# Linear attention and two squared-ReLU layers on one core: waits for finished weights, a sum of copies on DVE, operands moved by 16 bytes

## The chip, the cores and the metric

One core of a Trainium2 chip runs the kernel. The metric is the time of one execution on the device in microseconds: 1520.22 us is the median of three runs of the kernel before (1519.58 to 1520.62).

## The reference

Attention with a softmax over the head dimension of q and over the sequence of k, then two feed-forward layers. Inputs are float32: q, k, v of 8 x 8 x 576 x 64, and for each layer w_in of 512 x 2048 and w_out of 2048 x 512.

```python
q_s = softmax(q, axis=-1)
k_s = softmax(k, axis=2)
kv = np.einsum('bhsd,bhse->bhde', k_s, v)
x = np.einsum('bhsd,bhde->bhse', q_s, kv)
x = x.transpose(0, 2, 1, 3).reshape(4608, 512)
h = np.maximum(x @ w_in, 0.0)
x = h * h @ w_out
r = np.maximum(x @ w_in2, 0.0)
return r * r @ w_out2
```

## The kernel before, in words

**Tiling.** The 4608 tokens are 9 blocks of 512 (`NB`). The four matrix products are four stages one after the other: stage 0 takes attention and the first w_in, block by block; stage 1 the first w_out; stage 2 the second w_in; stage 3 the second w_out. Hidden activations go to DRAM and come back as tiles G. Each fp32 operand is split into a rounded high part and the rest, and each product is three matmuls: low by high, high by low, high by high (`passes`, L437 to L442; every such matmul has line L441).

**Seven products.** In stage 0 from the seventh block on (`FIRST = 6`), and in stages 1 to 3, the blocks of a product are combined by sums into seven products instead of eight (`LEFT`, `RIGHT`, `ORDER`). One operand tile then holds 2 x 7 pieces of 256 columns: seven high, seven low. `first_mm` (L450) makes the products of stages 0 and 2, whose outputs the trace calls n and m: a unit is seven products of 12 matmuls, and product 2 comes first and is the only one that reads piece 0 of the moving operand (`RIGHT[2] = 0`). There are four units in a block. `second_mm` (L498) makes those of stages 1 and 3 (both are y): 42 matmuls for each of eight parts a of each block. In stage 1 the weights W are stationary and G moves; in stage 3 G is stationary and W moves.

**Addresses.** Tiles whose name begins with G, x or v have 48 spare words, and `comb_hi` (L108) starts the pieces at a word offset in them: `PLAIN` 8 as a rule, `EARLY` 4 for `G0_0_0` and for the first x block, `LATE` 40 for all tiles G of stage 3 and 44 for its first two. A word is 4 bytes. The tile v is the moving operand of the seventh to ninth blocks in stage 0.

**After the products.** `first` (L986) joins the seven: ACT copies products 2 and 5 out of PSUM (`copy`, L468), POOL adds the two copies (`both`, L471), DVE subtracts the sum from product 1 (`rest`, L474), and the rest follows by `plain`, `summed`, `relu` and `square`. `second` (L1039) uses `both` and `rest` as well.

**Who decides the order.** All steps are made as operations with an engine, a cost and a due time; `schedule` (L594) simulates them, each engine taking the ready operation with the earliest due time whose tiles are free, and the resulting order is the program: every engine works through its own instructions in that order, and SP issues nearly all DMAs from one queue. A random search of 400 rounds moves due times of the first part only (up to a chunk of the third block). An `after` of the planner binds the chip only where the data do: a DMA that the planner puts behind another transfer for reasons of traffic alone waits for nothing on the chip.

**Weights.** For 13 parts the finished operand (1792 KB) is written to DRAM early (`keep`) and read back by `get_operand` (L183) from POOL's queue. `behind` (L794) names, for four of these reads, a load of activations that the planner puts ahead: `(2, 2)` and `(2, 3)` behind the last G of stage 1, `(3, 5)` and `(3, 7)` behind the fifth and the seventh G of stage 3. `load_g` (L494) reads G, `load_y` (L535) reads the output of stage 1 as xq, `load_raw` (L129) reads unconverted weights, and `between` (L1113) makes the x of stage 2, on POOL from the third block on.

Of the kernel before, what the change touches and what calls it, by code (L numbers as in the profile page):

```python
# [9 lines left out]
F32 = mybir.dt.float32  # L10
# [11 lines left out]
P = 128  # L22
# [26 lines left out]
def linear_attention_two_relu2_ffn(ctx: ExitStack, tc: tile.TileContext, q0, k0, eye, qh, kh, vh, wio, out):  # L49
# [27 lines left out]
    def f32(ap):  # L77
        return ap.bitcast(F32)
# [11 lines left out]
        return pool.tile([P, 2, HB], F32, name=name, tag=f"t{place.slot}")  # L90


    hls, cfs = {}, {}


    def comb_add(key, q, x, eng, new):
# [11 lines left out]
    def comb_hi(key, q, x, tag):  # L108
        if key not in hls:
            if key[0] in "Gxv":  # L110
                t = pool.tile([P, 14 * HB + SHIFT], F32R, name=key, tag=tag)
                o = LATE + 4 * (key in ("G1_0_0", "G1_0_1")) if key[:2] == "G1" else EARLY if key == "G0_0_0" or key[:2] == "x0" else PLAIN
                hls[key] = t[:, o:o + 14 * HB].rearrange("p (a b n) -> p a b n", a=2, b=7)
            else:
                hls[key] = pool.tile([P, 2, 7, HB], F32R, name=key, tag=tag)
        r, src = (slice(0, 2), q[:, 0:4:3]) if x == 0 else (slice(2, 7), cfs[key])
        nc.scalar.activation(out=hls[key][:, 0, r], in_=src, func=AF.Copy)  # L117

    def comb_lo(key, q, x):
        r, src = (slice(0, 2), q[:, 0:4:3]) if x == 0 else (slice(2, 7), cfs.pop(key))  # L120
        hl = hls[key]
        nc.vector.tensor_tensor(out=hl[:, 1, r], in0=src, in1=f32(hl[:, 0, r]), op=ALU.subtract)  # L122

# [53 lines left out]

    def put_operand(f, a):  # L180
        nc.sync.dma_start(out=ready_w[f, a], in_=f32(hls.pop(f"S{f}_{a}")))

    def get_operand(f, a, tag):  # L183
        hls[f"W{f}_{a}"] = pool.tile([P, 2, 7, HB], F32R, name=f"W{f}_{a}", tag=tag)
# [265 lines left out]
    def first_mm(l, j, u, i, place):  # L450

        k, o = (l, j, u), BANK[i]
        if i == o:
            m[k, o] = bank(place, f"{'nm'[l]}{i}_{j}_{u}")
        for s in range(2):
            w = hls[f"W{2 * l}_{2 * u + s}"]
            terms = []
            for kk in range(2):
                x, c = hls[f"{'vx'[l]}{j}_{kk}"], slice(kk * P, (kk + 1) * P)
                terms.append((w[:, 0, LEFT[i], c], w[:, 1, LEFT[i], c], x[:, 0, RIGHT[i]], x[:, 1, RIGHT[i]]))  # L460
            passes(m[k, o][:, s], terms, start=i == o and s == 0)

    def temp(k, i):
# [3 lines left out]
    def copy(k, i):  # L467
        nc.scalar.activation(out=temp(k, f"s{i}"), in_=m[k, i], func=AF.Copy)  # L468

    def both(k):  # L470
        nc.gpsimd.tensor_tensor(out=t[k, "s5"], in0=t[k, "s5"], in1=t[k, "s2"], op=ALU.add)  # L471

    def rest(k):
        nc.vector.tensor_tensor(out=t[k, "s5"], in0=m[k, 1], in1=t[k, "s5"], op=ALU.subtract)  # L474
# [71 lines left out]
    class Op:  # L546
        def __init__(self, eng, cost, due, fn, after, uses, lands, lag, port):
            self.eng, self.cost, self.due, self.fn, self.lands = eng, cost, due, fn, lands
            self.after = [a for a in after if a is not None]
            self.uses, self.lag, self.port = uses, lag, port  # L550
            self.start, self.group = None, group[0]
            self.next = []

    class Place:
# [33 lines left out]
    OVERLAP = {"DVE": 80, "ACT": 95, "POOL": 40}  # L588
    LAG, SLACK, HEAD, REST, COLD, SLOTS = 90, 1500, 110_000, 1600, 1400, {"t": TS, "ps": 8}

    def dma(due, fn, kb, after=(), uses=(), n=1):
        return op("SP", (570 if after else 390) * n, due, fn, after, uses, lands=kb)

    def schedule(moved, until=None):  # L594
        for o in ops:
# [17 lines left out]
        for x, o in enumerate(ops):  # L613
            o.rank = (o.due + moved.get(o.group, 0.0) + moved.get(x, 0.0), x)
            if not o.wait and (until is None or o.due < until.due + 60_000):
                push(0.0, "ready", o)
        done = []
        while events:
            now = events[0][0]
# [2 lines left out]
            while events and events[0][0] <= now:  # L622
                _, _, kind, what = heapq.heappop(events)
                if kind == "ready":
                    heapq.heappush(ready[what.eng], (what.rank, what))
                elif kind == "idle":
                    idle[what] = True
                else:
                    for x in what.uses:
                        x.users -= 1  # L630
                        if not x.users:
                            free[x.tag].append(x.slot)
                    for y in what.next:
                        y.wait -= 1

                        over = what.eng != y.eng or now < HEAD and any(b.eng != y.eng for b in y.after)
                        y.ready = max(y.ready, now + (LAG + y.lag if over else 0))
                        if not y.wait:
                            push(y.ready, "ready", y)
            for e, q in ready.items():  # L640
                held = []
                while idle[e] and q:
# [109 lines left out]
    def converted(f, a, h, due, raw, wf):  # L752

        (rp, rnew), (wp, wnew) = raw, wf
        l = dma(due - 8000, lambda: load_raw(f, a, h, rnew), 512, [], [rp])
        late = 2500 if f else 0
        c = op("ACT", act(512) + 40, due - 3000, lambda: low_word(f, a, h), [l], [rp], lag=late)
        g = op("DVE", 430, due - 2900, lambda: high_word(f, a, h), [l], [rp], lag=late, port=True)
        x = op("ACT", act(512) + 40, due - 1900, lambda: scaled(f, a, h, wnew), [g], [rp, wp])
        return op("DVE", 690, due - 700, lambda: join(f, a, h), [c, x], [rp, wp], port=True)  # L760
# [30 lines left out]
    def slot_of(a):  # L791
        return f"w{(a + 5) % 8}"

    g_loads, behind = {}, {(2, 2): (0, NB - 1, 7), (2, 3): (0, NB - 1, 7), (3, 5): (1, 0, 4), (3, 7): (1, 0, 6)}  # L794

    def weights(f, a, due):

        if (f, a) in KEPT:
            place = Place(slot_of(a))
            l = op("POOL", 1400, due - 9000, lambda: get_operand(f, a, slot_of(a)), [*kept[f, a], g_loads.get(behind.get((f, a))), begun.get((f, a))], [place], lands=1792, port=False)  # L800
            combined[f"W{f}_{a}"] = [l], place
            return
        beside = Place(slot_of(a + 1)) if f == 0 and a not in (2, 7) else None
# [182 lines left out]
    def first(l, j, u):  # L986
# [28 lines left out]
        c2 = copy_of(2, d + g)  # L1015
        mm(5, d + g, [M[2]])
        c5 = copy_of(5, d + 2 * g)
        s = op("POOL", gps(512), d + 3 * g, lambda: both(k), [c2, c5], [tt["s5"], tt["s2"]])
        mm(1, d + 4 * g, [M[5], *chain[-1:]])
        if (l, j, u) == (1, 0, 1):  # L1020
            begun[2, 7] = M[1]
# [65 lines left out]
    def hidden(l, j, a):  # L1087
# [13 lines left out]
        if n < 5 or n >= end - 6:  # L1101
            cf = cf_place(("cf", "att2")[n % 2])
        elif n % 3 == 2:
            cf = Place("cfx", parent=spare[l])
            cf = cf, lambda: spare[l].area(2048, 5 * HB).rearrange("p (a n) -> p a n", n=HB)
        else:
            cf = cf_place(("cf", "att2")[n % 3])
        y = g_loads[l, j, a] = dma(d - (30000 if n < 5 else 20000), lambda: load_g(l, j, a, new), 512, stored[l, j, a], [place])
        if l == 0:
            y = op("ACT", act(1024), d - 10000, lambda: g_square(j, a), [y], [place])  # L1110
# [2 lines left out]
    def between(j, kk):  # L1113
        d = when(2, j)
        tag = (("qx", "qa") if j == 0 else ("qc", "qd"))[kk]
        place = Place(tag)
        ld = dma(d - 20000, lambda: load_y(j, kk, tag), 512, [y_stored[(0, j), q] for q in range(4)], [place])
        combine(f"x{j}_{kk}", f"hl{(2 * j + kk + 3) % 4}", d - 10000 + 5000 * kk, ("DVE" if j < 2 else "POOL",) * 3, lambda: xq[j, kk], place, [ld], *cf_place("att1" if j == 0 else ("cf", "att2")[kk]))

    for j in range(NB):  # L1120
# [103 lines left out]
```

## Time and profile before

| what | value |
|---|---|
| median of three runs | 1520.22 us (1519.58 to 1520.62) |
| the profiled execution's own time | 1531.24 us |
| its span | 1529.4 us |
| PE busy | 1503.5 us (98%) |
| DVE, ACT, POOL busy | 1192.1, 966.5, 253.1 us |
| mean granted TensorE clock | 0.999 |

The span runs from the first to the last instruction; the execution's own time is 1.84 us longer. The profiled execution is 11.0 us longer than the median of the runs. Engine times overlap: the sum over engines says nothing, and an engine that is not on the path may wait at no cost. A row of the timeline gives start, duration, engine, line, operation, tiles, count, and in brackets the idle time ahead of it with what ended it.

### The profile page before, as it was taken

The page shows a single profiled execution, that of the slowest core. Times are in us where ns is not written, and L with a number is a line of the kernel's source. Part 1 is how long each engine was busy: PE and PEld are TensorE (multiplying, and loading weights), DVE is VectorE, ACT ScalarE, POOL GpSimd, SP SyncE. Part 2 cuts the span into 40 slices and gives each one's busy share as a digit, 9 for nine tenths or more (in the row PEclk, how much of TensorE's full clock was granted, in tenths as well). Part 3 has the DMA queues.
Part 4 walks back from the last instruction along what each step waited for, and adds up shares of the span by engine and source line. Part 5 has one row for each costly group of instructions (what it writes and reads, how often), then busy time and mean ns, then how long its engine had stood idle before and what let it go on. Part 6 is the DMA issues. An engine that isn't in the chain of part 4 may idle for free.

```text
span 1529.4 us, 30550 instructions
## 1 busy us (share of the span) xinstructions
PE 1503.5 (98%) x12036; PEld 1428.4 (93%) x12036; DVE 1192.1 (78%) x1819; ACT 966.5 (63%) x1617; POOL 253.1 (17%) x193
## 2 busy tenths in 40 slices
PE   7999999999999999999999999999999999999998
PEld 5788888889899999999998999999999999999998
DVE  7998777797977999999987544444455998898885
ACT  8987666686866666666555777777776434334332
POOL 1000000001110111111112433333211111111110
PEclk9999999999999999999999999999999999999999
DMA  9888999985669544444357767767659444433441
GB/s 371 291 294 314 345 322 323 346 277 195 194 208 327 175 140 139 138 139 139 123 203 287 242 216 229 244 205 236 222 171 359 160 134 130 136 129 130 137 128 46
DMA packets 154143, 326.63 MB, mean 214 GB/s; under 512 B 13072, under 2 KB 84880, under 8 KB 151184
## 3 DMA queue, kind: packets, MB, share of 16 engines
q1 hardware_dynamic: 152128, 300.83, 58.8%
q0 software_dynamic: 1872, 23.86, 4.2%
q8 instruction: 94, 1.54, 0.4%
q14 instruction: 49, 0.40, 0.1%
HBM read 189.63 MB, written 135.00 MB: 212 GB/s over the span
## 4 chain that ended last, share of the span: by engine, by line
PE 86%; issue 5%; DVE 3%; DMA 3%; ACT 3%; POOL 0%; SPq 0%; DVEq 0%; ACTq 0%; POOLq 0%
PE y L441 41%; PE m L441 21%; PE h L441 15%; PE n L441 6%; PE xps L398 1%; DMA xq<-y 1%; PE kvps L327 1%; DMA g<-t 1%; POOL ts L471 0%; ACT wf L159 0%; ACT w L150 0%; DMA w<-wio 0%; DMA w<-k 0%; DVE wf L164 0%; ACT w L215 0%
## 5 line engine op out<-in xcount | busy, mean ns | idle before, releaser
L441 PE MATMUL y<-W,G 128*128 128x256 f32 x3024 | 355.8, 281 | 1.2 <-DVE ts L474 1.2
L441 PEld LDWEIGHTS y<-W,G 128*128 128x128 f32 x3024 | 355.3, 189 | 1.4 <-DVE ts L474 1.4
L441 PE MATMUL m<-x,W 128*128 128x256 f32 x3024 | 345.8, 277 | 1.5 <-ACT ts L468 1.5
L441 PEld LDWEIGHTS m<-x,W 128*128 128x128 f32 x3024 | 345.1, 188 | 1.9 <-ACT ts L468 1.9
L441 PE MATMUL y<-G,W 128*128 128x256 f32 x3024 | 344.2, 276 | 2.2 <-DVE G L122 2.2
L441 PEld LDWEIGHTS y<-G,W 128*128 128x128 f32 x3024 | 343.4, 188 | 2.6 <-DVE G L122 2.6
L441 PE MATMUL h<-hl,w 128*128 128x512 f32 x1080 | 259.8, 396 | 3.4 <-DVE w L84 3.4
L441 PEld LDWEIGHTS h<-hl,w 128*128 128x128 f32 x1080 | 200.4, 188 | 49.6 <-DVE w L84 5.7
L471 POOL TENSOR_TENSOR ts<-ts,ts 128x512 f32<-128x512 f32 x65 | 100.6, 1548 | 782.5 <-DVE t L510 450.0
L117 ACT ACTIVATE G<-hl 128x1280 fp32r<-128x1280 f32 (+1 forms) x95 | 86.1, 925 | 120.9 <-PE y L441 61.6
L480 DVE TENSOR_TENSOR t<-m,ts 128x512 f32<-128x512 f32 x72 | 48.9, 688 | 116.2 <-PE m L441 89.4
L441 PE MATMUL n<-v,W 128*128 128x256 f32 x1008 | 124.5, 285 | 3.0 <-ACT t L477 3.0
L441 PEld LDWEIGHTS n<-v,W 128*128 128x128 f32 x1008 | 121.1, 191 | 5.9 <-ACT t L477 4.2
L122 DVE TENSOR_TENSOR G<-hl,G 128x512 fp32r<-128x512 f32 (+1 forms) x95 | 109.9, 1160 | 20.3 <-ACT G L117 19.1
L483 ACT ACTIVATE t<-t 128x512 f32<-128x512 f32 x96 | 59.6, 627 | 59.3 <-DVE t L480 58.1
L486 ACT ACTIVATE t<-t 128x512 f32<-128x512 f32 x144 | 88.8, 627 | 1.9
L122 DVE TENSOR_TENSOR G<-cf,G 128x1280 fp32r<-128x1280 f32 x51 | 79.7, 1563 | 7.7 <-ACT G L117 7.0
L122 DVE TENSOR_TENSOR G<-att,G 128x1280 fp32r<-128x1280 f32 x49 | 76.7, 1565 | 8.8 <-ACT G L117 8.3
L312 POOL PARTITION_ALL_REDUCE m<-m x28 | 26.2, 935 | 305.3 <-DVE m L308 156.9
L428 ACT ACTIVATE r<-h 128x512 f32<-128x512 f32 x96 | 56.7, 592 | 21.7 <-PE h L441 16.3
L117 ACT ACTIVATE G<-cf 128x1280 fp32r<-128x1280 f32 x51 | 64.4, 1263 | 7.7 <-DVE cf L106 7.7
L513 POOL TENSOR_TENSOR t<-t,t 128x512 f32<-128x512 f32 x34 | 62.1, 1849 | 42.1 <-DVE t L480 42.1
(195 smaller groups left out, 1880.6 us busy)
## 6 DMA issues: line engine op xcount, KB each, us to landing
g<-t SPq DMA_DIRECT2D x192, 256.0 KB, 4.0
hl<-g SPq DMA_DIRECT2D x51, 512.0 KB, 3.7
raw<-wio SPq DMA_DIRECT2D x48, 512.0 KB, 5.1
g<-r SPq DMA_DIRECT2D x96, 256.0 KB, 5.2
W<-o POOLq DMA_DIRECT2D x13, 1792.0 KB, 9.7
y<-t SPq DMA_DIRECT2D x72, 256.0 KB, 2.4
w<-wf SPq DMA_DIRECT2D x64, 256.0 KB, 5.4
o<-S SPq DMA_DIRECT2D x9, 1792.0 KB, 8.3
```

The lines of the kernel that those rows point to most:

```text
L117: nc.scalar.activation(out=hls[key][:, 0, r], in_=src, func=AF.Copy)
L122: nc.vector.tensor_tensor(out=hl[:, 1, r], in0=src, in1=f32(hl[:, 0, r]), op=ALU.subtract)
L312: nc.gpsimd.partition_all_reduce(m[:, 1, :P], m[:, 0, :P], P, bass.bass_isa.ReduceOp.max)
L327: nc.tensor.matmul(ps[j * D:(j + 1) * D, 0:D + 1], k[lo:, c, j * D:(j + 1) * D], v[lo:, c, j, :], start=(c == 0), stop=(c == KC - 1),)
L398: nc.tensor.matmul(ps[:, r], begin[b % 2][p], q[:, r], start=True, stop=True)
L428: nc.scalar.activation(out=r0[j, f].rearrange("p a b -> p (a b)"), in_=m.pop(("h", j, f)), func=AF.Relu)
L441: nc.tensor.matmul(ps, a, b, start=start, stop=True, skip_group_check=True)
L471: nc.gpsimd.tensor_tensor(out=t[k, "s5"], in0=t[k, "s5"], in1=t[k, "s2"], op=ALU.add)
L480: nc.vector.tensor_tensor(out=temp(k, q), in0=m[k, i], in1=t[k, "s5"], op=ALU.add)
L483: nc.scalar.activation(out=t[k, q], in_=t[k, q], func=AF.Relu)
L486: nc.scalar.activation(out=t[k, q], in_=t[k, q], func=AF.Square)
L513: nc.gpsimd.tensor_tensor(out=t[k, q], in0=t[k, q], in1=t[k, o], op=ALU.add)
```

## The change

Five things. (1) In the seventh block `both` runs on DVE in place of POOL. (2) For the tiles v, high pieces 0 are written and read 16 bytes lower than the plain place; piece 1 and all others stay (`low`). (3) The tile `G1_2_0` (part 0 of the third block of stage 3) gets the word offset 44 in place of 40. (4) For the four reads in `behind`, POOL first adds two words of the G tile that was loaded (`touch`), so that the read of the weights, behind it on POOL's queue, is issued when that G has landed. (5) In the planner, the loads of the second and third x block and of the raw weights of part 0 of stage 3 are not ready before a fixed planned time (`held`).

```diff
         if key not in hls:
             if key[0] in "Gxv":
-                o = LATE + 4 * (key in ("G1_0_0", "G1_0_1")) if key[:2] == "G1" else EARLY if key == "G0_0_0" or key[:2] == "x0" else PLAIN
+                o = LATE + 4 * (key in ("G1_0_0", "G1_0_1", "G1_2_0")) if key[:2] == "G1" else EARLY if key == "G0_0_0" or key[:2] == "x0" else PLAIN
                 hls[key] = t[:, o:o + 14 * HB].rearrange("p (a b n) -> p a b n", a=2, b=7)
+                if key[0] == "v":
+                    low[key] = t[:, o - 4:o - 4 + 2 * (HB + 4)].rearrange("p (a n) -> p a n", a=2)[:, :, :HB]
...
-        nc.scalar.activation(out=hls[key][:, 0, r], in_=src, func=AF.Copy)
+        nc.scalar.activation(out=low[key] if x == 0 and key in low else hls[key][:, 0, r], in_=src, func=AF.Copy)
...
-        nc.vector.tensor_tensor(out=hl[:, 1, r], in0=src, in1=f32(hl[:, 0, r]), op=ALU.subtract)
+        hi = low[key] if x == 0 and key in low else hl[:, 0, r]
+        nc.vector.tensor_tensor(out=hl[:, 1, r], in0=src, in1=f32(hi), op=ALU.subtract)
...
+    def touch(f, a, key):
+        one = pool.tile([P, 1], F32, name=f"touch{f}_{a}", tag="kvm")
+        nc.gpsimd.tensor_tensor(out=one, in0=gq[key][:, 0, 0:1], in1=gq[key][:, 0, 0:1], op=ALU.add)
...
-                terms.append((w[:, 0, LEFT[i], c], w[:, 1, LEFT[i], c], x[:, 0, RIGHT[i]], x[:, 1, RIGHT[i]]))
+                high = x[:, 0, RIGHT[i]] if l or RIGHT[i] else low[f"v{j}_{kk}"][:, 0]
+                terms.append((w[:, 0, LEFT[i], c], w[:, 1, LEFT[i], c], high, x[:, 1, RIGHT[i]]))
...
-    def both(k):
-        nc.gpsimd.tensor_tensor(out=t[k, "s5"], in0=t[k, "s5"], in1=t[k, "s2"], op=ALU.add)
+    def both(k, eng="POOL"):
+        (nc.gpsimd if eng == "POOL" else nc.vector).tensor_tensor(out=t[k, "s5"], in0=t[k, "s5"], in1=t[k, "s2"], op=ALU.add)
...
-    def dma(due, fn, kb, after=(), uses=(), n=1):
-        return op("SP", (570 if after else 390) * n, due, fn, after, uses, lands=kb)
+    def dma(due, fn, kb, after=(), uses=(), n=1, held=None):
+        o = op("SP", (570 if after else 390) * n, due, fn, after, uses, lands=kb)
+        o.held = 0.0 if held is None else due - held
+        return o
...
-                push(0.0, "ready", o)
+                push(max(0.0, o.held), "ready", o)
...
-                            push(y.ready, "ready", y)
+                            push(max(y.ready, y.held), "ready", y)
...
-        l = dma(due - 8000, lambda: load_raw(f, a, h, rnew), 512, [], [rp])
+        l = dma(due - 8000, lambda: load_raw(f, a, h, rnew), 512, [], [rp], held=10000 if (f, a) == (3, 0) else None)
...
-            l = op("POOL", 1400, due - 9000, lambda: get_operand(f, a, slot_of(a)), [*kept[f, a], g_loads.get(behind.get((f, a))), begun.get((f, a))], [place], lands=1792, port=False)
+            b = behind.get((f, a))
+            if b:
+                assert b in g_loads, (f, a)
+            seen = op("POOL", 200, due - 9000, lambda: touch(f, a, b), [g_loads[b]], [g_place[b]]) if b else None
+            l = op("POOL", 1400, due - 9000, lambda: get_operand(f, a, slot_of(a)), [*kept[f, a], seen, begun.get((f, a))], [place], lands=1792, port=False)
...
-        s = op("POOL", gps(512), d + 3 * g, lambda: both(k), [c2, c5], [tt["s5"], tt["s2"]])
+        if (l, j) == (0, FIRST):
+            s = op("DVE", dve(512), d + 3 * g, lambda: both(k, "DVE"), [c2, c5], [tt["s5"], tt["s2"]], port=True)
+        else:
+            s = op("POOL", gps(512), d + 3 * g, lambda: both(k), [c2, c5], [tt["s5"], tt["s2"]])
...
-        ld = dma(d - 20000, lambda: load_y(j, kk, tag), 512, [y_stored[(0, j), q] for q in range(4)], [place])
+        ld = dma(d - 20000, lambda: load_y(j, kk, tag), 512, [y_stored[(0, j), q] for q in range(4)], [place], held=8000 if j in (1, 2) else None)
```

## Rows read from the trace of the kernel before

**Rows 1.** The page's first part: busy time of each engine.

```profile
PE 1503.5 (98%) x12036; PEld 1428.4 (93%) x12036; DVE 1192.1 (78%) x1819; ACT 966.5 (63%) x1617; POOL 253.1 (17%) x193
```

**Rows 2.** Windows, PE alone: stretch, length, busy (matmuls), clock, DMA share, GB/s.

```profile
425.00:473.00 48.00, 48.00 (x410) 1.00 0.71 227
484.00:804.00 320.00, 320.00 (x2826) 1.00 0.48 158
...
1220.00:1500.00 280.00, 280.00 (x2379) 1.00 0.41 131
```

**Rows 3.** Windows, PE alone, of four short stretches in stages 2 and 3.

```profile
845.00:860.00 15.00, 15.00 (x128) 1.00 0.89 294
870.00:885.00 15.00, 15.00 (x135) 1.00 0.74 240
1173.00:1178.00 5.00, 5.00 (x44) 1.00 0.96 264
1179.00:1184.00 5.00, 5.00 (x47) 1.00 1.00 407
```

**Rows 4.** Waits of PE in the seventh block: total, times, longest.

```profile
PE n L441 <- ACT t L477: 3.0, 3, 1.9
PE xps L398 <- DVE qT L391: 0.6, 1, 0.6
```

**Rows 5.** Timeline of the first unit of the seventh block, all engines.

```profile
342.81 1.81 POOL L312 PARTITION_ALL_REDUCE m<-m  x1 [9.09 <-ACT r L428]
...
347.55 0.60 ACT L468 ACTIVATE ts<-n 128x512 f32<-128x512 f32 x1
...
353.91 1.26 POOL L471 TENSOR_TENSOR ts<-ts,ts 128x512 f32<-128x512 f32 x1 [9.29 <-issue]
...
355.21 0.69 DVE L474 TENSOR_TENSOR ts<-n,ts 128x512 f32<-128x512 f32 x1 [6.54 <-POOL ts L471]
...
357.96 3.26 PE L441 MATMUL n<-v,W 128*128 128x256 f32 x14 [1.88 <-ACT t L477]
```

**Rows 6.** Windows, all engines, of the seventh block; PEclk, DMA share and GB/s last.

```profile
342.00:362.00 20.00, 18.12 (x160) 17.01 (x159) 13.00 (x24) 10.81 (x19) 3.64 (x3) 0.91 0.60 204
362.00:402.00 40.00, 38.29 (x311) 35.22 (x311) 35.77 (x66) 31.56 (x73) 5.59 (x5) 1.00 0.59 186
```

**Rows 7.** Groups by form: a DVE sum of 128x512 from SBUF.

```profile
L102 DVE TENSOR_TENSOR cf<-qc 128x512 f32<-128x512 f32 x22 | 15.1, 685 | 2.8 <-DMA qc<-w 2.0 <-DMA qc<-g 0.4 <-ACT qc L435 0.2
```

**Rows 8.** Timeline around the step from stage 1 to stage 2, all engines.

```profile
795.67 0.53 POOL L185 DMA_DIRECT2D W<-o  x1 [4.23 <-PE y L441]
...
796.93 0.32 SPq L496 DMA_DIRECT2D qe<-g  x1
...
801.62 5.83 SPq L537 DMA_DIRECT2D xq<-y  x2
...
813.58 1.06 ACT L435 ACTIVATE qe<-qe 128x1024 f32<-128x1024 f32 x1 [4.88 <-DMA qe<-g]
...
816.96 1.65 PE L441 MATMUL y<-G,W 128*128 128x256 f32 x12 [1.01 <-DVE G L122]
...
819.77 3.56 PE L441 MATMUL y<-G,W 128*128 128x256 f32 x29 [1.16 <-DVE G L122]
...
824.27 14.57 PE L441 MATMUL m<-x,W 128*128 128x256 f32 x120 [0.95 <-ACT ts L468]
```

**Rows 9.** Timeline of the weight reads on POOL, stage 2 to stage 3.

```profile
1173.40 0.53 POOL L185 DMA_DIRECT2D W<-o  x1 [10.57 <-DMA g<-t]
```

**Rows 10.** The page's DMA issues: weight reads, KB each, median us to landing.

```profile
W<-o POOLq DMA_DIRECT2D x13, 1792.0 KB, 9.7
```

**Rows 11.** Timeline of PE at the start of stage 3.

```profile
1172.82 37.84 PE L441 MATMUL y<-W,G 128*128 128x256 f32 x330
1211.84 13.34 PE L441 MATMUL y<-W,G 128*128 128x256 f32 x111 [1.18 <-DVE ts L474]
```

**Rows 12.** The tile xq: landing times of its 18 loads.

```profile
DMA to landing us min/median/max: 3.5/4.1/20.9
```

More of the change, by code (lines that the diff above doesn't have):

```diff
@@ L90, in two @@
         return pool.tile([P, 2, HB], F32, name=name, tag=f"t{place.slot}")
-    hls, cfs = {}, {}
+    hls, cfs, low = {}, {}, {}
     def comb_add(key, q, x, eng, new):
@@ L550, in __init__ @@
             self.uses, self.lag, self.port = uses, lag, port
-            self.start, self.group = None, group[0]
+            self.start, self.group, self.held = None, group[0], 0.0
             self.next = []
@@ L792, in slot_of @@
         return f"w{(a + 5) % 8}"
-    g_loads, behind = {}, {(2, 2): (0, NB - 1, 7), (2, 3): (0, NB - 1, 7), (3, 5): (1, 0, 4), (3, 7): (1, 0, 6)}
+    g_loads, g_place, behind = {}, {}, {(2, 2): (0, NB - 1, 7), (2, 3): (0, NB - 1, 7), (3, 5): (1, 0, 4), (3, 7): (1, 0, 6)}
     def weights(f, a, due):
@@ L1107, in hidden @@
             cf = cf_place(("cf", "att2")[n % 3])
+        g_place[l, j, a] = place
         y = g_loads[l, j, a] = dma(d - (30000 if n < 5 else 20000), lambda: load_g(l, j, a, new), 512, stored[l, j, a], [place])
```

## The prediction

> **What bounds the kernel now.** I read the engines' busy time first. PE is busy 98% of the span [rows 1], so only two things can shorten it: the pace of a matmul, and the stalls between them. Next I read windows of PE alone, inside stretches without a stall, for the pace: length divided by matmuls. In stage 1 from 484 us it is 320/2826 = 113.2 ns; in the last two blocks of stage 0 it is 48/410 = 117.1 ns; in stage 3 from 1220 us it is 280/2379 = 117.7 ns [rows 2]. The shapes are the same and the granted clock is 1.00 in all three. So there are **two paces, some 4.4 ns apart**, and 10,000 matmuls of this shape run at one or the other.
>
> What switches them? The order of the parts in the code gives the places. In stage 2 the first block of x stands at word 4 and later ones at word 8: 15/128 = 117.2 ns in the first block, 15/135 = 111.1 in the second. In stage 3 the first two tiles G stand at word 44 and the third at 40: 5/44 = 113.6 and 5/47 = 106.4 ns [rows 3]. Short windows count cut matmuls at both ends, so only the difference is to be read; it points the same way both times. A step of the moving operand up by 16 bytes, or of the stationary one down by 16, is followed by the quick pace. The timeline at the start of stage 3 shows how it is lost: 330 y matmuls after 1172.82, then a stall of 1.18 us for DVE's `rest` [rows 11], and 1220 to 1500 is slow.
>
> Then the stalls, by PE's waits and the timelines. The seventh block has 3.0 + 0.6 us of waits [rows 4] and a window at a mean clock of 0.91 [rows 6]; the step from stage 1 to 2 has 1.01, 1.16 and 0.95 us [rows 8]; stage 3 has 1.18 [rows 11].
>
> **The change, part by part.**
>
> *Sum on DVE in the seventh block.* In the first unit ACT's second copy ends at 347.55 + 0.60 = 348.15, but POOL's sum starts at 353.91, after 9.29 us of idle time that no engine ends, and the instruction ahead of it is another kind, the all-reduce of 342.81. DVE stood 6.54 us for that sum, and PE 1.88 us [rows 5]. The row shows that the first sum after an all-reduce starts late. The Trainium skill, GPSIMD Engine Reference, section Instruction dispatch, says that a freshly loaded POOL kernel costs some 6 us of code loading; the row's 9.29 is longer and decides, and by 6 us the sum would have started some 3 us earlier and PE's stall would be nearly gone already. On DVE the sum is a step of 0.69 us [rows 7] right behind the copies. What goes: the first stall of 1.88 and the low clock after it. Mean 0.91 over 20 us is 3.6 us at the lower level, 1.2 GHz, half of it lost: 1.8 us. Together 3.7. The other waits, 3.0 + 0.6 - 1.9 = 1.7, come later in a stretch where DVE is busy 35.77 of 40 us [rows 6]; DVE gains up to 6.54 us of a lead and pays 4 x 0.685 = 2.74 for four sums, so a part of them goes too: I take 0.5 of 1.7. Sum **4.2 us**, bounds 2.0 (a late DVE takes half) and 5.4. POOL's own queue loses four sums; its all-reduces are no later for that.
>
> *First operand 16 bytes lower.* In v's units, product 2 is at the lower place, the other six are not, so each unit holds one step up. By the two steps of [rows 3] the 72 matmuls that follow should be quick, until a matmul of attention or a stall comes between. Of 12 units I count eight as free of these: 8 x 72 x 4.4 ns = 2.5 us; I take **2.3**. Product 2 itself mixes both places; its 12 matmuls per unit lie between the two paces, so nothing to 0.6 us lost (144 x 4.4). Bounds: 0 (a step in one piece of the operand does nothing) and 3.9 (72 x 12 units). The writes of ACT and reads of DVE are as long as before and cost nothing.
>
> *Reads of weights wait; loads held.* Before, the read of 795.67 goes out ahead of the last G of stage 1, whose load is issued at 796.93 and reaches ACT at 813.58, after ACT stood 4.88 us for it; PE then waits 1.01 and 1.16 for that G, and 0.95 for a copy that ACT makes late [rows 8]. With the touches, this read and the next stand on POOL's queue behind that G; with the hold, the loads xq of 801.62 leave the stretch. Behind the touch on POOL only further weight reads wait there. They are 1792 KB each, 9.7 us to landing [rows 10]: issued at about 805 they are there by 820 for two of them, and product 2 of the second unit of stage 2 wants them some 7 us after the 824 of [rows 8]. A touch itself is one tiny add: between 0 and the 1.26 of a 128x512 sum [rows 5], hidden, since POOL stands there. If that cover is gone, a G is late by as much. The gain is 1.01 + 1.16 + 0.95 = 3.1 at most; late next is DVE, which has the adds of the next operands to do. I take **2.8**, bounds 0 and 3.8 (a further short stall in the first block of stage 2).
>
> *The same at stage 3.* The read of 1173.40 [rows 9] has to wait for a G issued at about the same time; the tile that it fills is used some 28 us later (six parts of 42 x 113.2 ns), so 5 us more are hidden. Fewer bytes in that stretch let G land and DVE run earlier, which is where the 1.18 comes from. I take **0.6**, bounds 0 and 1.2.
>
> *G1_2_0.* The step from 44 to 40 comes at its end. The slow stretch holds 3024 - 366 = 2658 matmuls at 4.5 ns more: **11.9 us** in the profiled execution, of which the step gives back 2310 x 4.5 = 10.4.
>
> **Against which time?** The profiled execution took 1531.24 (a span of 1529.4 and 1.84 around it), the median of the runs is 11.0 lower. Take the slow stretch out and 1531.24 - 11.9 = 1519.3 is left, beside runs of 1519.6 to 1520.6. So I read it thus: the timed runs kept the quick pace through stage 3, and there G1_2_0 has nothing to give back. The sum for the profiled execution is 4.2 + 2.3 + 2.8 + 0.6 + 11.9 = 21.8, to 1509.4; for the median it is 4.2 + 2.3 + 2.8 + 0.6 = 9.9, to **1510.3**.
>
> **Rivals.**
>
> *The runs were slow in stage 3 as well* (the 11.0 us are the cost of profiling). Then 10.4 to 11.9 come on top: 1510.3 - 11.2 = 1499. For it: one stall of 1.18 us is in the code's order and should be in every run. Against it: the match of 1519.3.
>
> *The address does nothing* (the pace follows the stalls' phase and not the operands). Then 2.3 is missing: 1512.6; if half of the stalls also stay, 1516. For it: the quick pace also begins without a step elsewhere, and two steps are few. The Trainium skill, SBUF — State Buffer, section Specifications (TRN2), speaks of 16-byte lines, where crossing a line costs; a move by a whole line should change nothing by that. The two steps of [rows 3] speak against that rule.
>
> *The held x comes late* (slower). The hold puts the load of the second x block at the planner's 830.2 us (858.2 for its block less 20 and 8). Its adds and splits take about 8 us, and PE wants it near 860, or 3 us sooner with the gain of that step. A landing of 4.1 leaves 14 us; one of 20.9, which happened once [rows 12], leaves a stall of 1 us, eats the 2.8, and can start the slow pace with no further step in stage 2: some 2500 matmuls x 4.4 = 11 us. Result 1510.3 + 2.8 + 1 + 11 = 1525. The point that decides: whether the last DVE split of that x ends before about 858.
>
> *It doesn't do what it says*: the reordered queues bring new stalls of the size removed, 1518 to 1521.
>
> **How the numbers follow.** A measurement here can tell about 0.2%, 3.0 us, from no change. Chances: forecast 0.50, runs slow in stage 3 before 0.25, address does nothing 0.12 (two thirds of it faster by over 0.2%), new stalls 0.07 (0.06 the same, 0.01 slower), held x late 0.06. Faster 0.50 + 0.25 + 0.08 = 0.83; the same 0.04 + 0.06 = 0.10; slower 0.07. The forecast's own bounds are 1505 to 1516; the range reaches to the first rival, 1498, and to 1517.
>
> **What would show it.** Right: no `both` on POOL before the eighth block, DVE's 6.54 us idle gone, clock 1.00 from 342 to 362; pace 113 in most of 425 to 473; the last G of stage 1 at ACT before 808 and no PE wait for it; no stall at 1210; pace 113 from the third block of stage 3. Wrong: pace 117 behind the lower piece; the time falling by about 20 us; a stall near 860 with slow matmuls behind it.

## The result and the profile after

The changed kernel takes **1508.22 us** (median of ten runs, 1507.41 to 1519.81), the kernel before 1520.48 beside it (ten runs, 1519.31 to 1531.55): a ratio of 0.9913 [0.9889, 0.9937], 12.3 us less where 9.9 were forecast. The two profiled executions are further apart, 1531.24 and 1511.11, by 20.1 us where 21.8 were forecast. Both kernels have a few executions some 11 us above their others; of the 99 timed runs of the kernel before in this study 28 lie above 1527 and 71 at 1522.6 or below. The profiled one of before was of the upper kind, that of after was not, and this is why the profiles differ by more than the medians.

The page of after, its first part:

```profile
PE 1487.6 (99%) x12036; PEld 1414.4 (94%) x12036; DVE 1190.4 (79%) x1823; ACT 971.0 (64%) x1617; POOL 253.6 (17%) x193
```

PE's count is that of [rows 1] and its busy time is 15.9 us shorter: most of the 20.1 us between these two profiles is pace. This says nothing of the 12.3 us between the medians. By PE's waits, those of [rows 4] for ACT's t and for qT are gone, and two new ones of 2.0 and 1.5 us are there; both are shown below.

The first unit of the seventh block in the timeline of after, beside [rows 5]:

```profile
342.29 1.81 POOL L319 PARTITION_ALL_REDUCE m<-m  x1 [9.27 <-ACT r L435]
...
347.39 0.60 ACT L476 ACTIVATE ts<-n 128x512 f32<-128x512 f32 x1
...
348.02 0.69 DVE L479 TENSOR_TENSOR ts<-ts,ts 128x512 f32<-128x512 f32 x1 [0.24 <-ACT ts L476]
...
349.37 0.68 DVE L482 TENSOR_TENSOR ts<-n,ts 128x512 f32<-128x512 f32 x1
...
354.68 3.57 PE L448 MATMUL n<-v,W 128*128 128x256 f32 x29
```

The sum starts 0.03 us behind ACT's copy where POOL's stood until 353.91, `rest` follows 5.8 us earlier than before, and PE has no stall there.

Windows of PE alone in after, beside [rows 2, 3]; the last three lie ahead of, in and behind the tile G1_2_0 of stage 3:

```profile
342.00:362.00 20.00, 20.00 (x188) 1.00 0.76 239
...
425.00:473.00 48.00, 47.37 (x413) 1.00 0.68 234
484.00:804.00 320.00, 320.00 (x2826) 1.00 0.47 152
845.00:860.00 15.00, 15.00 (x129) 1.00 0.49 158
870.00:885.00 15.00, 15.00 (x135) 1.00 0.68 205
1220.00:1490.00 270.00, 270.00 (x2382) 1.00 0.41 131
...
1225.00:1235.00 10.00, 10.00 (x91) 1.00 0.31 107
1238.00:1243.00 5.00, 5.00 (x44) 1.00 0.39 126
1245.00:1255.00 10.00, 10.00 (x91) 1.00 0.46 143
```

The first of these three in before, where stage 3 is slow:

```profile
1225.00:1235.00 10.00, 10.00 (x87) 1.00 0.32 107
```

The clock of 342 to 362 is 1.00 in place of 0.91. The stretch from 425 runs at 47.37/413 = 114.7 ns, with both paces in each unit, in place of 117.1; stage 3 runs at 270/2382 = 113.4 in place of 117.7; stages 1 and 2 are as before. In stage 3 the pace is quick from the second tile's end, slow in G1_2_0 (5/44 = 113.6 in a short window, beside 10/91 = 109.9 on both sides; such windows count cut matmuls, so only the difference is read), and quick again to the end. So stage 3 of after was quick before it came to G1_2_0, and that tile had no lost pace to give back.

The step from stage 1 to 2 in after, beside [rows 8], in the timeline of all engines:

```profile
802.98 1.04 ACT L442 ACTIVATE qe<-qe 128x1024 f32<-128x1024 f32 x1
...
804.11 7.57 POOL L188 TENSOR_TENSOR touch<-qe 128x1 f32<-128x1 f32 x2 [16.90 <-ACT qe L442]
...
809.87 1.48 DVE L125 TENSOR_TENSOR G<-att,G 128x1280 fp32r<-128x1280 f32 x1
...
811.45 4.93 PE L448 MATMUL y<-G,W 128*128 128x256 f32 x42
...
811.71 1.64 POOL L192 DMA_DIRECT2D W<-o  x3
...
824.27 6.95 PE L448 MATMUL m<-x,W 128*128 128x256 f32 x56 [1.45 <-DMA W<-o]
```

The last G reaches ACT 10.6 us earlier than before (802.98, 813.58; 5.9 of this were gained ahead of the main run of stage 1), and the 42 y matmuls of its part run without the stalls of 1.01 and 1.16. But the touch, two adds of one word per partition, takes 7.57 us, and three weight reads go out at 811.71 in a row; PE waits 1.45 us for one of them.

Where PE stands at the same instruction in the two profiles, by PE's timelines: the main run of y in stage 1 starts 5.9 us earlier (480.32, 474.42); the long run of m at the start of stage 2 8.1 (824.27, 816.22); the main run of y in stage 3 7.2 (1172.82, 1165.58); the last matmul ends 20.25 earlier (1525.16, 1504.91). So 13.0 of the 20.25 come in stage 3: the stall of 1.18 and 2658 x 4.5 = 12.0 of pace.

The 5.9 holds a loss. The timeline of after at 474, all engines, and the window of PE behind it:

```profile
469.30 0.69 DVE L102 TENSOR_TENSOR att<-qx 128x512 f32<-128x512 f32 x1 [5.95 <-DMA qx<-w]
...
473.68 1.28 DVE L488 TENSOR_TENSOR t<-n,ts 128x512 f32<-128x512 f32 x2
...
474.42 5.85 PE L448 MATMUL y<-G,W 128*128 128x256 f32 x35 [2.05 <-DVE t L488]
```

```profile
474.40:478.40 4.00, 3.98 (x20) 0.57 0.88 258
```

DVE waited 5.95 us for a weight (2.3 in e6, 2.2 in e8), then did the sums of that weight ahead of the t that PE wants. PE stood 2.05 us, and the next 4 us were granted 0.57 of the clock, near the lower of the two levels (1.2 GHz): 1.7 us more. This is 3.8 us of the profiled execution. The stall is 0.7 us in e3 below and absent in the profiles of e1, e2 and e4 to e8, of which e2, e5, e6 and e7 change addresses alone, so it belongs to some executions; the profiled time lies 2.9 us above the median.

### The profile page after: what moved, and what is told of

It is laid out like the page before. It is cut to its first block, busy times and chain, and to the rows that moved or that the text cites. A ratio compares the mean times of both kernels' runs of the same rounds, so it can differ in the third digit from the quotient of the medians.

```text
span 1509.3 us, 30549 instructions
## 1 busy us (share of the span) xinstructions
PE 1487.6 (99%) x12036; PEld 1414.4 (94%) x12036; DVE 1190.4 (79%) x1823; ACT 971.0 (64%) x1617; POOL 253.6 (17%) x193
## 4 chain that ended last, share of the span: by engine, by line
PE 90%; DMA 3%; ACT 3%; DVE 2%; issue 1%; POOL 1%; SPq 0%; DVEq 0%; ACTq 0%; POOLq 0%
PE y L448 44%; PE m L448 22%; PE h L448 15%; PE n L448 5%; PE xps L405 2%; PE kvps L334 1%; DMA qx<-w 1%; DMA W<-o 1%; POOL touch L188 0%; ACT w L153 0%; ACT wf L162 0%; DMA w<-w 0%; DMA w<-wio 0%; DMA qc<-w 0%; DMA att<-vh 0%
## 5 line engine op out<-in xcount | busy, mean ns | idle before, releaser
L448 PE MATMUL y<-W,G 128*128 128x256 f32 x3024 | 343.9, 276 | 0.0
L448 PEld LDWEIGHTS y<-W,G 128*128 128x128 f32 x3024 | 343.7, 188 | 0.0
L479 POOL TENSOR_TENSOR ts<-ts,ts 128x512 f32<-128x512 f32 x61 | 93.5, 1533 | 750.2 <-DVE t L518 460.4
L448 PE MATMUL n<-v,W 128*128 128x256 f32 x1008 | 120.3, 280 | 0.0
L448 PEld LDWEIGHTS n<-v,W 128*128 128x128 f32 x1008 | 117.1, 188 | 2.1 <-issue 1.7
```

The source lines that it names most:

```text
L448: nc.tensor.matmul(ps, a, b, start=start, stop=True, skip_group_check=True)
L479: (nc.gpsimd if eng == "POOL" else nc.vector).tensor_tensor(out=t[k, "s5"], in0=t[k, "s5"], in1=t[k, "s2"], op=ALU.add)
```

## The experiments

Each is the changed kernel with the edit shown, unless said otherwise. Ratios are to the kernel before, run alongside. Differences to 1508.22 are differences of medians, of runs at another time; those under 3 us are less than the intervals tell apart.

**e1: the sum back on POOL.**

```diff
-        if (l, j) == (0, FIRST):
+        if False:
```

> The changed kernel with one part undone: in the seventh block the sum of copies is on POOL again. Theory (the first sum after an all-reduce starts some 9 us late): POOL's first sum there starts about 6 us behind the second copy, DVE stands about 6 us for it, PE stalls 1 to 2 us in the first unit and the clock falls; the time is 3 to 5 us above the changed kernel, about 1512. Rival (DVE's idle time was covered, and the seventh block is bound by something else): within 1 us of the changed kernel, 1508.

Measured: 1513.61 (1512.39 to 1515.5, ten runs), 0.993 [0.9905, 0.9955], 5.4 more. The timeline of POOL and of ACT's copy, then the window of PE and one of its waits between 340 and 402:

```profile
342.06 1.81 POOL L319 PARTITION_ALL_REDUCE m<-m  x1 [9.19 <-ACT r L435]
...
346.93 0.60 ACT L476 ACTIVATE ts<-n 128x512 f32<-128x512 f32 x1
...
354.11 1.27 POOL L479 TENSOR_TENSOR ts<-ts,ts 128x512 f32<-128x512 f32 x1 [10.24 <-issue]
...
370.70 0.99 POOL L319 PARTITION_ALL_REDUCE m<-m  x1 [7.77 <-DVE m L315]
380.10 1.28 POOL L479 TENSOR_TENSOR ts<-ts,ts 128x512 f32<-128x512 f32 x1 [8.41 <-issue]
```

```profile
342.00:362.00 20.00, 17.95 (x173) 1.00 0.55 189
```

```profile
PE xps L405 <- ACT begin L353: 1.8, 2, 1.2
```

The late sum is back, a second all-reduce is followed by a second one, and the waits for t come back with 3.1 us, 2.04 of them in the first unit. With 1.8 for ACT's writes of the tile `begin`, 0.7 for qT and 0.2 for DVE's t, PE waits 5.8 us between 340 and 402, in after 0.4. The clock was expected to fall and did not: it stays 1.00. The waits' difference, 5.8 - 0.4, is that of the times, 5.4.

**e2: the first piece of v at the plain place.**

```diff
-                if key[0] == "v":
+                if False:
...
-                high = x[:, 0, RIGHT[i]] if l or RIGHT[i] else low[f"v{j}_{kk}"][:, 0]
+                high = x[:, 0, RIGHT[i]]
```

> The changed kernel with one part undone: piece 0 of v at the plain place. Theory (a step up of the moving operand by 16 bytes brings the quick pace): the last two blocks of stage 0 run at about 117 ns a matmul in place of 113 to 114, time 2 to 3 us above the changed kernel, about 1510.5. Rival (the pace follows the stalls; without stalls the quick pace comes anyway): 113 to 114 ns and the changed kernel's 1508.

Measured: 1509.78 (1509.51 to 1511.27, seven runs), 0.9913 [0.988, 0.9945], 1.6 more. **e7: every piece of v lower**, so that no step of address is left inside a unit:

```diff
-                o = LATE + 4 * (key in ("G1_0_0", "G1_0_1", "G1_2_0")) if key[:2] == "G1" else EARLY if key == "G0_0_0" or key[:2] == "x0" else PLAIN
+                o = LATE + 4 * (key in ("G1_0_0", "G1_0_1", "G1_2_0")) if key[:2] == "G1" else EARLY if key == "G0_0_0" or key[:2] == "x0" or key[0] == "v" else PLAIN
...
-                if key[0] == "v":
+                if False:
...
-                high = x[:, 0, RIGHT[i]] if l or RIGHT[i] else low[f"v{j}_{kk}"][:, 0]
+                high = x[:, 0, RIGHT[i]]
```

> The changed kernel with all pieces of v 16 bytes lower, not piece 0 alone: the places are as low, but there is no step within a unit. Theory (the step counts, not the place): last two blocks of stage 0 at 117 ns or slower, time 2 to 3 us above 1508, as with all pieces at the plain place. Rival (the lower place is the quick one): 113 ns throughout, 1507.5.

Measured: 1511.09 (1510.49 to 1512.4, eight runs), 0.9927 [0.9897, 0.9957], 2.9 more. One window of PE in e1 (where the lower piece is left in), e2 and e7:

```profile
425.00:465.00 40.00, 40.00 (x352) 1.00 0.71 218
```

```profile
425.00:465.00 40.00, 40.00 (x342) 1.00 0.61 199
```

```profile
425.00:465.00 40.00, 40.00 (x338) 1.00 0.60 197
```

113.6, 117.0 and 118.3 ns a matmul: the lower place alone gives nothing (it is the slowest of the three), the step between two places does. The times of e2 and e7 by themselves lie too close to the changed kernel's to tell; the windows do.

**e5 and e6: stage 3 without a step, and with the steps turned round** (36 and 40 in place of 44 and 40).

```diff
-                o = LATE + 4 * (key in ("G1_0_0", "G1_0_1", "G1_2_0")) if key[:2] == "G1" else EARLY if key == "G0_0_0" or key[:2] == "x0" else PLAIN
+                o = LATE if key[:2] == "G1" else EARLY if key == "G0_0_0" or key[:2] == "x0" else PLAIN
```

and in e6

```diff
+                o = LATE - 4 * (key in ("G1_0_0", "G1_0_1", "G1_2_0")) if key[:2] == "G1" else EARLY if key == "G0_0_0" or key[:2] == "x0" else PLAIN
```

> The changed kernel with all tiles G of stage 3 at word 40: no step of the stationary operand in that stage. Theory (the quick pace comes by a step of the stationary operand down by 16 bytes, and word 40 is not quick by itself): stage 3 runs at 117 to 118 ns a matmul from its start, 3000 x 4.4 ns = 13 us more, about 1521. Rival (place 40 is quick and 44 slow, whatever was before): 113 ns and 1508. Third (the pace after a change of operands is chance): one or the other, and differing between runs.

> The changed kernel with the three tiles G that stand at word 44 at word 36 instead: the step at their end is 16 bytes up, not down. Theory (the direction counts): slow behind each step, stage 3 at 117 to 118 ns, about 1521. Rival (any step of 16 bytes does it): quick from the third part on, 1508.

Measured: e5 1520.03 (1518.93 to 1522.04, eight runs), 0.9974 [0.994, 1.0008], 11.8 more; e6 1506.66 (two runs), 0.9878 [0.9799, 0.9957]. Windows of PE in e5, then in e6:

```profile
1175.00:1195.00 20.00, 20.00 (x172) 1.00 0.45 165
1245.00:1490.00 245.00, 245.00 (x2082) 1.00 0.40 131
```

```profile
1245.00:1490.00 245.00, 245.00 (x2164) 1.00 0.39 128
```

Without a step all of stage 3 is slow (117.7), and all eight runs of e5 are as long; with steps the other way it is quick (113.2; two runs, one profile). So here the addresses decide the pace, and the direction of the step doesn't matter. e5 takes away the step behind the first two tiles too, which before has as well, so it doesn't tell what G1_2_0 is worth.

**e3, e4 and e11: touches and holds taken away.** e3 has no touch (the first of the three edits), e4 no hold (the second and third), e11 neither (all three).

```diff
-            seen = op("POOL", 200, due - 9000, lambda: touch(f, a, b), [g_loads[b]], [g_place[b]]) if b else None
+            seen = g_loads[b] if b else None
...
-        l = dma(due - 8000, lambda: load_raw(f, a, h, rnew), 512, [], [rp], held=10000 if (f, a) == (3, 0) else None)
+        l = dma(due - 8000, lambda: load_raw(f, a, h, rnew), 512, [], [rp], held=None)
...
-        ld = dma(d - 20000, lambda: load_y(j, kk, tag), 512, [y_stored[(0, j), q] for q in range(4)], [place], held=8000 if j in (1, 2) else None)
+        ld = dma(d - 20000, lambda: load_y(j, kk, tag), 512, [y_stored[(0, j), q] for q in range(4)], [place], held=None)
```

> The changed kernel without the four adds on POOL: the reads of weights again wait for nothing on the chip; the loads stay held. In the profile of the changed kernel the first of these adds lasted 7.3 us, until DVE paused, and PE later stood 1.45 us for a read of weights. Theory (the touch keeps the last G of stage 1 early and is worth 2 to 3 us, less the 1.45): that G reaches ACT some 5 us later than in the changed kernel, PE waits 1 to 2 us for it, no wait for a read of weights; time 0 to 2 us above 1508. Rival (the hold alone empties the stretch): G is in time, the 1.45 us are gone, time about 1.5 us below, 1506.5.

> The changed kernel without the planner's hold on the loads of the second and third x block and of the raw weights; the touches stay. Theory (touch and hold both empty the stretch before stage 2): the loads xq go out before the last G of stage 1 lands or right behind it, reads of weights land later, PE's wait for them grows from 1.45 to 3 us or more; time 1 to 3 us above 1508. Rival (the hold does nothing): 1508 and the same 1.45.

> The changed kernel without touches and without holds. Theory (the two work only together: one keeps the last G early, the other takes bytes out of the stretch): the step from stage 1 to stage 2 has the stalls of the kernel before, some 3 us, and stage 3 a stall of 1 us; time 3 to 5 us above 1508, about 1512. Rival (they cancel: the touch's own lateness costs what it saves): 1508 to 1509.

Measured: e3 1511.56 (1509.56 to 1524.19, ten runs), 0.9928 [0.9898, 0.9958]; e4 1513.9 (1513.05 to 1518.21, ten), 0.9935 [0.9906, 0.9965]; e11 1513.85 (1511.19 to 1526.8, ten), 0.9963 [0.9934, 0.9993]. PE's waits in e3, and the timeline of all engines in e4:

```profile
PE y L448 <- DVE G L125: 2.3, 2, 1.2
...
PE y L448 <- DVE ts L482: 1.1, 1, 1.1
```

```profile
800.92 10.79 POOL L188 TENSOR_TENSOR touch<-qe 128x1 f32<-128x1 f32 x2 [17.02 <-ACT qe L442]
...
820.85 0.95 PE L448 MATMUL m<-x,W 128*128 128x256 f32 x6 [2.07 <-DMA W<-o]
825.65 6.61 PE L448 MATMUL m<-x,W 128*128 128x256 f32 x40 [3.85 <-DMA W<-o]
```

Without touches the last G is late again (2.3 us), and so is `rest` in stage 3 (1.1 us at 1202; no such wait in the profiles with touches). Without holds the touch is longer, because DVE has the sums of xq to do as well, and the loads of xq share the stretch with three weight reads: 5.9 us of waits, and a clock of 0.50 from 825 to 829 behind them. By the medians, touches without holds are worth nothing (1513.9 against 1513.85), holds alone 2.3, both 5.6; e3 and e4 lost more than was expected. The profile of e11, the fastest of its ten runs, shows waits of 2.3, 1.5 and 0.5 us at these places, 2.9 more than after's 1.45; where the rest of the 5.6 went is not shown.

**e8: the touch on ACT**, a copy of one word of G into the tile that the read then fills.

```diff
...
-        nc.gpsimd.tensor_tensor(out=one, in0=gq[key][:, 0, 0:1], in1=gq[key][:, 0, 0:1], op=ALU.add)
+        hls[f"W{f}_{a}"] = pool.tile([P, 2, 7, HB], F32R, name=f"W{f}_{a}", tag=slot_of(a))
+        nc.scalar.activation(out=hls[f"W{f}_{a}"][:, 0, 0, 0:1], in_=gq[key][:, 0, 0:1], func=AF.Copy)
...
-            seen = op("POOL", 200, due - 9000, lambda: touch(f, a, b), [g_loads[b]], [g_place[b]]) if b else None
+            seen = op("ACT", 220, due - 9000, lambda: touch(f, a, b), [g_loads[b]], [g_place[b], place]) if b else None
```

> The changed kernel with the touch on ACT: ACT copies one word of G into the first word of the tile that the weights are read into, in place of POOL's add, so that the read waits for ACT. Theory (POOL's first add was held up for 7.3 us by DVE's sums of two SBUF operands, and that made the reads late): the reads that wait for the last G of stage 1 go out near 804 in place of 811.7, PE's wait of 1.45 us for weights is gone, the last G is as early as before; time 1 to 2 us below 1508. Rival (the reads are late for their bytes, not for the add): they go out earlier but PE waits as long; 1508.

Measured: 1507.1 (1505.31 to 1509.26, four runs), 0.9886 [0.9824, 0.9947], 1.1 less. The timeline of ACT's touch and of POOL's reads, then the only wait of PE at this step:

```profile
799.46 0.20 ACT L188 ACTIVATE W<-qe 128x1 fp32r<-128x1 f32 x1
...
801.13 1.60 POOL L193 DMA_DIRECT2D W<-o  x3 [18.51 <-PE y L449]
```

```profile
PE m L449 <- ACT t L486: 0.2, 1, 0.2
```

The reads go out 10.6 us earlier than in after, 4.6 of it because that G reaches ACT earlier (798.38, 802.98), the rest because the touch takes 0.20 us and not 7.30. PE's wait for a read is gone. So the touch itself was what made the reads late. The gain is less than the runs can tell.

**e9 and e12: more steps, on top of e8.** e9 puts the first x at the plain place with its piece 0 lower. e12 adds a lower piece 0 in part 1 of every block of stages 1 and 3 (not `G1_0_1`), to win the quick pace back after any stall; the first two of the edits below are e9's, the third e12's; the lines that read the lower piece are left out.

```diff
-                o = LATE + 4 * (key in ("G1_0_0", "G1_0_1", "G1_2_0")) if key[:2] == "G1" else EARLY if key == "G0_0_0" or key[:2] == "x0" else PLAIN
+                o = LATE + 4 * (key in ("G1_0_0", "G1_0_1", "G1_2_0")) if key[:2] == "G1" else EARLY if key == "G0_0_0" else PLAIN
...
-                if key[0] == "v":
+                if key[0] == "v" or key[:2] == "x0":
...
-                if key[0] == "v" or key[:2] == "x0":
+                if key[0] == "v" or key[:2] == "x0" or key[0] == "G" and key[4:] == "_1" and key != "G1_0_1":
```

> The kernel with the touch on ACT, and the first x block of stage 2 changed as v was: only piece 0 stands 16 bytes lower, the others at the plain place. In the changed kernel that block stands lower as a whole and runs at 119.2 ns. Theory (one lower piece per unit is enough to start the quick pace, in stage 2 as in stage 0): the first block of stage 2 runs near 114 ns, 288 matmuls x 5.9 ns = 1.7 us less; with ACT's touch 2 to 4 us below the changed kernel's 1508.2, about 1505. Rival (the block lost nothing, or the step is lost at the stalls there): as with the touch on ACT alone, 1507.

> The kernel of the run before last but two (touch on ACT, one lower piece in the first x block) with one piece 16 bytes lower also in part 1 of every block of stages 1 and 3 (12 matmuls of two parts' worth of products are touched in all but the first block of stage 3). Theory (a stall of PE as short as 0.2 us at a change of blocks can start the slow pace, and a stage without a step stays slow to its end): each block gets the quick pace back within its first two parts, 5 us at the most are lost to one stall instead of up to 13; all runs near 1505, none above 1509. Rival (the slow pace has another cause than stalls, or one lower piece does nothing in these stages): some runs of 1515 to 1519 as before.

Measured: e9 1506.17 (1504.38 to 1519.16, eight runs), 0.9921 [0.9887, 0.9956]; five runs lie from 1504.38 to 1506.33, three from 1515.91 to 1519.16. e12 1512.54 (1510.9 to 1514.76, twelve), 0.9929 [0.9905, 0.9952]. The window of PE over stage 1 in e9, whose profiled execution is one of the three, and its loads of weights just ahead; then three blocks of stage 1 in e12:

```profile
484.00:804.00 320.00, 320.00 (x2720) 1.00 0.43 145
```

```profile
473.13 27.04 PEld L449 LDWEIGHTS y<-G,W 128*128 128x128 f32 x229 [0.22 <-DVE t L490]
```

```profile
510.00:550.00 40.00, 40.00 (x342) 1.00 0.46 159
550.00:589.00 39.00, 39.00 (x347) 1.00 0.41 135
589.00:629.00 40.00, 40.00 (x342) 1.00 0.43 136
```

The first block of stage 2 is nearly quick in e9 (218 matmuls from 820 to 845, 114.7 ns), but stage 1 is slow in that execution from its start, 117.6 all through, behind a wait of 0.22 us at 473. In e12 each lower piece of stage 1 turned the pace over: 117.0, 112.4, 117.0. Its expectation missed: the twelve runs lie within 4 us, but some 7 us above the 1505 that was expected, and in the profiled one half of stage 1 is slow.

**e10: the kernel before, with G1_2_0 at 44 and nothing else.**

```diff
-                o = LATE + 4 * (key in ("G1_0_0", "G1_0_1")) if key[:2] == "G1" else EARLY if key == "G0_0_0" or key[:2] == "x0" else PLAIN
+                o = LATE + 4 * (key in ("G1_0_0", "G1_0_1", "G1_2_0")) if key[:2] == "G1" else EARLY if key == "G0_0_0" or key[:2] == "x0" else PLAIN
```

> The kernel before with one edit alone: the first part of the third block of stage 3 at word 44. So far 62 timed runs of the kernel before fell into two groups, near 1520 and near 1531. Theory (a stall of PE at the start of the second block of stage 3 leaves stage 3 slow in some executions, and a step gives the quick pace back in all): all runs in 1518 to 1523, none near 1531. Rival (the two groups have another cause, in DMA or in the start): runs near 1530 stay.

Measured: 1520.62 (1519.67 to 1530.36, ten runs, three of them from 1528 up), 1.001 [0.9987, 1.0033]. So the expectation missed: runs near 1530 stay. The profiled execution took 1530.36; PE's loads and windows:

```profile
557.22 2.89 PEld L441 LDWEIGHTS y<-G,W 128*128 128x128 f32 x24 [0.17 <-DVE ts L474]
```

```profile
560.00:800.00 240.00, 240.00 (x2040) 1.00 0.40 130
850.00:868.00 18.00, 18.00 (x153) 1.00 0.88 289
884.00:924.00 40.00, 40.00 (x355) 1.00 0.65 209
1255.00:1490.00 235.00, 235.00 (x2073) 1.00 0.42 140
```

Here stage 3 is quick (113.4) and stage 1 is slow (117.6): the pace changes at 557.22, behind a wait of 0.17 us at a change of block. Out of this slow stage 1, the first x block of stage 2, at word 4, runs at 117.6 too, and the blocks behind it, at word 8, at 112.7. Stage 3 was quick ahead of G1_2_0 here as well (91 matmuls from 1225 to 1235). So the upper group isn't made by stage 3 alone: a stage that runs at the slow pace makes an execution some 10 us longer.

## Why the prediction was right or wrong

The sign and the size held, and the parts that the runs took out add up: 5.4 (e1) + 1.6 (e2) + 5.6 (e11) = 12.6 beside 12.3 measured. That they do so to 0.3 us is in part luck, since each is known to some 3 us. The terms were not each right: the first and the third were too small, the second, as far as the runs can tell, too large, and in the first and the last the mechanism was another than the prediction's.

- **Sum on DVE, 4.2.** That POOL's sum is late and that this costs PE held; e1 gives 5.4, the term's upper bound. What the sum is made of did not. Its second part, "1.8 us" for "the low clock after it", is not in e1: there the stall is back with 2.04 us and the clock stays 1.00, as it does from 342 to 362 in e10, whose sum is on POOL too. So the low clock of before belongs to that execution. And "I take 0.5 of 1.7" was too small: 3.8 of the 5.8 us of waits in e1 come behind the first stall, and in after the later waits for t and qT went completely (PE busy 39.60 of the 40 us from 362). That the two errors cancel is luck. The 9.29 us of idle time are not the lateness either: 3.53 of them pass until ACT's second copy ends at 348.15, and POOL's sum starts 5.76 us behind that copy, 6.58 in e1.
- **First operand lower, 2.3.** The runs give 1.6 (e2), within its bounds but less than they can tell; the windows show the pace, and e7 that the step counts and not the place. The window read as "the last two blocks of stage 0", 425 to 473, holds about one and a quarter. The rule behind the term fell: "a step of the moving operand up by 16 bytes, or of the stationary one down by 16, is followed by the quick pace". e6 is quick with the steps the other way. What fits the whole tiles is this: a tile that stands 16 bytes off the plain place is slow itself (G1_2_0 in after, the first x block in e10, all of v in e7), and the tiles behind it at the plain place are quick, whether the stretch ahead was quick (stage 1 in after) or slow (stage 1 in e10). The one exception found is stage 1 of e9: its first tile stands 16 bytes lower too, and it is slow behind a wait of 0.22 us.
- **Touches and holds, 2.8 + 0.6.** They are worth 5.6 by the medians, above the 3.8 + 1.2 of the two upper bounds. The three stalls of [rows 8] went as predicted, and so did the 1.18 of [rows 11]. Two steps failed. The price of a touch, 0 to 1.26 and "hidden, since POOL stands there", was wrong: the touch took 7.57 us, the reads went out at 811.7 and not "at about 805", and the predicted slack turned into a wait of 1.45. And the hold was costed with the touch as one term, though its own worth depends on it: touches alone give nothing, and the reads and the loads of xq then meet (e4, 5.9 us of waits).
- **G1_2_0, 11.9 and nothing.** The 11.9 is there between the profiles, but it isn't G1_2_0's. The step that failed is "the step from 44 to 40 comes at its end", with which 10.4 of it come back: after is quick already ahead of that tile (91 matmuls from 1225 to 1235, before 87), and the tile only made its own 42 matmuls slow. After did not lose the pace at 1210, where the stall of 1.18 is gone. That the stall's going kept the pace is not shown: e3, e10 and e11 have it, with 1.11, 1.70 and 0.51 us, and stay quick. No profile has a stage 3 that is slow ahead of G1_2_0, and no run takes this edit alone out of the changed kernel, so whether it can give a lost pace back is open. In before, the step alone brings nothing in the median (e10), as was forecast. That the usual runs of before are quick in stage 3 was argued from 1531.24 - 11.9 = 1519.3; the 99 runs show the two groups that this asks for. No profile of a usual execution of before was taken, so this is supported, not seen.
- **Rivals and bounds.** That the runs were slow in stage 3 as well fell by the median. That the address does nothing fell by e5 and by the windows of e1, e2 and e7. The held x was not late: no wait near 860. New stalls did come, 1.45 us at 824 and 2.05 us with its clock at 474, but smaller than what went; the second was not foreseen at all. It comes of DVE's order, a weight's sums ahead of the t that PE wants, in executions in which that weight lands late. The terms' lower bounds add up to 2.0 us, which is 1518 and not the 1516 given as the forecast's own bound.

Open is why a step or a stall changes the pace. In stage 1 of e12 a lower piece turned it over once per block, in stage 3 of the same run the same edit left it quick (window 1255 to 1490: 235/2074 = 113.3); the stalls of 1.70 us in e10 and 1.11 in e3 at the start of the second block of stage 3 left it quick and the one of 1.18 in before didn't. In stage 1, waits of 0.17 us (e10) and 0.22 (e9) stand ahead of the slow pace, waits of 0.7 (e3) and 2.05 (after) ahead of the quick one. What decides this was not found.

No run beats the changed kernel by more than can be told: e8 by 1.1, e6 by 1.6 in two runs, e9 by 2.05 in the median, with three of eight runs 8 to 11 us above 1508.22.

## What to carry to other kernels

Count the pace of the matmuls in windows without a stall before hunting stalls: 4.4 ns on 2700 matmuls are 12 us here, as much as e5 lost in every run, and waits of 0.2 us stood at the start of such a loss in two executions. An edit that orders transfers has to be priced together with the one that clears their stretch, and an instruction that exists only to wait has to be priced on the engine that it stands on: ACT's one-word copy took 0.2 us where POOL's add took 7.3. When a profile is far from the median of the runs, ask which of its stretches the other runs don't have, and before crediting an edit with a stretch that is quick, look whether it was quick ahead of the edit's place.

## What was not expected of the hardware

**POOL held up by DVE.** The first touch of after ran from 804.11 to 811.40 for one word per partition; the tile's row of durations, and that of e4:

```profile
L188 POOL TENSOR_TENSOR touch<-qe x2: 193/3745/7297, 804.1 to 811.5; 128x1 f32<-128x1 f32 x2
L188 POOL TENSOR_TENSOR touch<-qd x1: 183/183/183, 1137.2 to 1137.2; 128x1 f32<-128x1 f32 x1
```

```profile
L188 POOL TENSOR_TENSOR touch<-qe x2: 193/5358/10523, 800.9 to 811.5; 128x1 f32<-128x1 f32 x2
```

Alone it takes 0.18 us. In after, DVE went from one sum with both inputs in SBUF to the next without a gap until 809.87 + 1.48 = 811.35, and the touch ended at 811.40. In e4 DVE had more such sums, and the touch ended at 811.44, when DVE's first sum with an input from PSUM had started (t from y, at 811.30). The Trainium skill, SBUF — State Buffer, section Who interferes with whom, says that VectorE and GpSimd share one pair of ports under an exclusive lock; the traces agree, and add that the one that waits can stay out for a whole chain of DVE's instructions, 7.3 and 10.5 us, not one of them. No run moved DVE's sums alone, so the lock as the cause rests on these ends and on e8.

**Two paces at one clock.** 113.3 and 117.7 ns for the same matmul at a granted clock of 1.00 in every stretch, and 118.3 where all of an operand stands 16 bytes lower (e7). A step of 16 bytes in an operand's address sets the pace (e5, e6, e12), and in some executions the slow one begins behind a wait as short as 0.17 us (e10) or 0.22 us (e9).

**POOL's change of kind.** The first sum after an all-reduce starts late, each time again, though its operands are there: 5.76 us behind ACT's second copy [rows 5], 6.58 behind it in e1, and 6.84 at the second all-reduce of e1 (copy from 372.66 to 373.26). POOL's idle time, 9.29, 10.24 and 8.41 us, holds the wait for the copy as well.
